# The seven products of the second channel product in transposed form, two of four sums per instruction, and small constants in shared space

## The chip, the cores and the metric

The kernel runs on one core of a Trainium2 chip (trn2). A core has a matrix engine (PE, with its weight loads shown apart as PEld), a vector engine (DVE), an engine for activation functions (ACT), a general engine (POOL), a queue engine (SP) and 16 DMA engines. The metric is the device time of one execution in microseconds (us); lower is better. A time is the median of several runs.

## What is computed

Two layers follow one another, for each of 8 batches (sequence S = 3008, width D = 256):

```
scores = (z @ z.T) / S                       # z: 3008 x 64
x  = u * (relu(scores)**2 @ v)               # u, v: 3008 x 256
h  = relu(x.T @ w_tok1) @ w_tok2             # w_tok1: 3008 x 256, w_tok2: 256 x 3008
u2 = x + h.T
out = u2 + relu(u2 @ w_ch1) @ w_ch2          # w_ch1: 256 x 1536, w_ch2: 1536 x 256
```

Inputs and output are float32 in memory; the products are taken in bf16 with float32 sums. The first channel product is `u2 @ w_ch1`, the second is `relu(...) @ w_ch2`.

## The kernel before

**Tiling.** The rows of a batch are cut into six blocks of 512 (the last has 448), called q; a block holds four tiles of 128 rows. Attention (`score_run`, `relu`, `square`, `av_matmul`) makes one block of scores after another: PE multiplies (L465), ACT takes the relu (L503), DVE squares (L511), and PE multiplies by v into `acc` (L692). Blocks of scores below the diagonal are not computed but obtained by turning the mirrored block with a transposing DMA on SP (L562, into buffers called `fl`). The result times u is `xT`.

**The mixer** of a batch (`add_mixer`) is a list of pieces: `tok1` (L1031) and `tok2` (L1105) for the token layer, `ch1` (L1162) for the first channel product, six pieces per block, each with 4 matmuls of 512 columns and one relu of 1024 columns on ACT (L1201) into `h2pre`, and `product` (L1298) for the second channel product.

**Seven products in place of eight.** The second channel product and the first token product use a scheme in which a 2x2 grid of sub-blocks is multiplied with seven products rather than eight, with sums of sub-blocks formed beforehand. For the second channel product the grid is: two interleaved sets of hidden columns (r) by two interleaved sets of row tiles (m). `make_sums` (L1227) forms, for each group d of four hidden tiles (three groups per block), four sums of relu outputs in `hsum`, each 512 elements per partition, with four DVE instructions: kind 0 (L1241), kind 2 (L1250), kind 1 (L1246, from kind 0), kind 3 (L1253, from kind 1). `mix_weights` (L975) forms four sums of w_ch2 once, in `w_mix_sb`. Each of the seven products is twelve matmuls of 128 columns (six where the block is short), into one of two PSUM banks: products 1, 6, 7, 4 go one after the other into the bank `xb`, and 2, 5, 3 into `zb`. After each, `collect` adds the bank to the output tile `ro` on DVE (L1334); products 6, 7, 4 wait for the addition of 1, 6, 7, and 5, 3 wait for that of 2, 5. Product 5 needs sum kind 0, 6 kind 1, 7 kind 2 and 3 kind 3; 1, 2 and 4 use plain relu outputs. For the token product `x_sums` (L904) forms four sums of x per block with four DVE instructions of 256 elements (L921); one of them overwrites part of x.

**Order of the work.** The program writes every engine's instruction order out by hand. A planner in the kernel (`push`, `run_engines`, the loop at the end) keeps a clock for PE, ACT, DVE and SP with an assumed cost for each operation, and takes at each step the piece that could start first; buffers are counted in `live` and `ROOM` (11 of `fl`, 6 of `h2`). Within a block the pieces of the second product are woven with the first product of the next block in the order 0, 0, 1, 2, 0, 6, 5, 0, 7, 3, 0, 4, where 0 is a `ch1` piece. The operations take their engine's queue in that order at run time, and PE executes in order: a matmul that waits holds all behind it. In the fourth block of all batches but the last the sums of two groups are held back (`late_sums`) and released together.

**Buffers the change touches.** `hsum` lies in an `fl` buffer (in early blocks an `at` buffer) and is given back after product 7. `a_f`, the token layer's first result in float32, lies in an `fl` buffer that is given back as soon as its relu is in `a_sb`, a constant tile. `ident`, a unit matrix for turning tiles on PE in the first 20 us, and `zs`, in which z is loaded, are constant tiles.

Of the kernel before, what the change touches and what calls it, by code (L numbers as in the profile page):

```python
# [57 lines left out]
def kernel(  # L58
# [38 lines left out]
    mark = consts.tile([P, 32], F32)  # L97
# [83 lines left out]
    def turn_on_pe(zr, zp):  # L181

        for t in range(GK):
            nc.tensor.matmul(  # L184
                zp[:, t, :], zr[:, t].rearrange("p h d -> p (h d)"), ident[:],
                start=(t == 0), stop=True, skip_group_check=True)
# [15 lines left out]
    def fill(n, bank):  # L202

        for _ in range(n):
            nc.tensor.matmul(
                bank, zero[:, :P], zero[:], start=True, stop=True, skip_group_check=True)
# [672 lines left out]
    def turn_x(b, q, t):  # L879

        if q % 2 == 0:
            x_pairs[b, q] = new_pair("fl" if b else "h2", [DT, QW // P, P], "x_pair")
        x = x_pairs[b, q - q % 2][:, q % 2]
        nc.sync.dma_start_transpose(
            out=x.rearrange("p h t d -> p (h t) d"),
            in_=xTs[b, q].rearrange("p h s -> p (h s)"))
        xs[b, q] = x
        x_done[b, q].t = t
        slack = 1.0 if b or q == NQ - 1 else 4.0 if q == NQ - 2 else 13.0
        push("dve", t + slack, 0.21, 0.36, lambda t: x_sums(b, q, t), first=-1,  # L890
             room=sums_room(b, q), frees=fl_free if xd_home(b, q) == "fl" and q % 2 == 0 else ())
# [16 lines left out]
    def x_sums(b, q, t):  # L908


        if q % 2 == 0:
            d_pairs[b, q] = new_pair(xd_home(b, q), [3, QW // P // 2, P], "d_pair")
        d = d_pairs[b, q - q % 2][:, q % 2]
        xds[b, q] = d
        v = xs[b, q].rearrange("p n (j r) d -> p n j r d", r=2)
        low, high = v[:, :, :, 0, :], v[:, :, :, 1, :]
        steps = [(d[:, 1], high[:, 1], low[:, 1]), (low[:, 1], low[:, 1], low[:, 0]),
                 (d[:, 0], high[:, 1], low[:, 1]), (d[:, 2], high[:, 0], d[:, 0])]

        def step(t):  # L920
            nc.vector.tensor_sub(*steps.pop(0))  # L921
# [52 lines left out]
    def mix_weights(t):  # L974


        w2 = w_ch2_sb.rearrange("p (j r) (h d) -> p j r h d", r=2, d=P)
        n = CHT // 4
        steps = []
        for c in range(2):  # L980
            low, high = w2[:, c * n:c * n + n, 0], w2[:, c * n:c * n + n, 1]
            to = w_mix_sb[:, :, c * n:c * n + n, :]
            steps += [
                (to[:, 0], low[:, :, 1, :], low[:, :, 0, :]),
                (to[:, 2], high[:, :, 1, :], low[:, :, 1, :]),
                (to[:, 1], high[:, :, 1, :], to[:, 0]),
                (to[:, 3], high[:, :, 0, :], to[:, 1])]

        def step(t):
            nc.vector.tensor_sub(*steps.pop(0))  # L990
# [4 lines left out]
        step(t)  # L995

    BORROW = 3
    VERY_LAST = (B - 1, NQ - 1, CHT // 2 - 1)
    ORDER_LAST = ((1, 2, 6, 5, 7, 0, 3, 4), (1, 2, 6, 5, 0, 7, 3, 0, 4))

    def add_mixer(b):
# [6 lines left out]
        def tok1(q, end):  # L1008
# [10 lines left out]
            for i in range(n):  # L1019
                j = q * n + i  # L1020
                products = [
                    ((0, 0), w[:, j, 0, 0, :], xp[:, 0, i, 0, :]),
                    ((0, 1), w[:, j, 1, 0, :], xp[:, 0, i, 1, :]),
                    ((1, 1), w[:, j, 0, 1, :], xp[:, 1, i, 0, :]),
                    ((0, 2), w_sum_sb[:, 1, j, :], d[:, 0, i, :]),
                    ((1, 2), w_sum_sb[:, 0, j, :], d[:, 1, i, :]),
                    ((0, 3), w_sum_sb[:, 2, j, :], xp[:, 1, i, 1, :]),
                    ((1, 0), w[:, j, 1, 1, :], d[:, 2, i, :]),
                ]
                for (r, k), lhs, rhs in products:  # L1030
                    nc.tensor.matmul(  # L1031
                        a_ps[:, r, k, :], lhs, rhs, start=(j == 0 and (r, k) in ((0, 0), (1, 1))),
                        stop=(j == KT // 2 - 1), skip_group_check=True)
# [3 lines left out]
            if q == NQ - 1:  # L1037
                home = "fl" if b else "h2"

                def collect_a(t):  # L1040
# [35 lines left out]
                    def relu_a(m, t):  # L1076
# [7 lines left out]
                        if len(made) == 2:  # L1084
                            recent[0] = to[:, :1]
                            if b:
                                release("fl", [1], max(made))
                            else:
                                live["h2"] -= 1

# [8 lines left out]
        def tok2(q, end):  # L1099
# [9 lines left out]
            def add(t):  # L1109
# [13 lines left out]
                u_done[q].t = t  # L1123
                st["turned", q] = push("sp", t, 1.25, 5.5, lambda t: turn_u2(q, t), first=1,
                                       room=lambda: has_room(("us",)) and (
                                           q <= HALF or goal[0] > (b, 1 + HALF)))
            ring.append((push("dve", end + 0.21, 1.12, 1.25, add, first=2), slot))

# [20 lines left out]
        def ch1(q, c2, borrowed, end):  # L1149
# [64 lines left out]
            if c2 == CHT // 2 - 1:  # L1214
                release("xT", xT_uses[q])

# [4 lines left out]
        def tiles_of(q, d, r, m):  # L1221

            n = pairs_of(q)
            return st["h2", q, d].rearrange("p (j r) w -> p j r w", r=2)[
                :, :, r, :2 * n * P].rearrange("p j (i m s) -> p j i m s", m=2, s=P)[:, :, :, m, :]

        def make_sums(q, d, t):  # L1227
# [6 lines left out]
            def kind(k):  # L1234
                return sums["s"][:, k, :, :n, :]

            def add1(t):
                home, n_home = take_home(q)
                sums["s"] = sb.tile([P, 4, 2, 2, P], BF16, tag=home, name="hsum", bufs=n_home)
                st["sum", q, d] = sums["s"]  # L1240
                nc.vector.tensor_add(kind(0), tiles_of(q, d, 0, 1), tiles_of(q, d, 1, 1))  # L1241
                push("dve", t - 0.05, busy, busy + 0.15, add3, done=s_done[q, d, 2])
                push("dve", t, busy, busy + 0.15, add2, done=s_done[q, d, 1])

            def add2(t):
                nc.vector.tensor_sub(kind(1), kind(0), tiles_of(q, d, 0, 0))  # L1246
                push("dve", t, busy, busy + 0.15, add4, done=s_done[q, d, 3])

            def add3(t):
                nc.vector.tensor_sub(kind(2), tiles_of(q, d, 0, 0), tiles_of(q, d, 0, 1))  # L1250

            def add4(t):
                nc.vector.tensor_sub(kind(3), tiles_of(q, d, 1, 0), kind(1))  # L1253

            push("dve", t, busy, busy + 0.15, add1, room=(home_of(q),), frees=frees_of(q),
# [16 lines left out]
        def product(q, k, end):  # L1272
# [6 lines left out]
            if k == 2:  # L1279
# [6 lines left out]
            weights = {1: w2[:, :, 0, 0, :], 2: w2[:, :, 1, 0, :], 3: w2[:, :, 1, 1, :],  # L1286
                       4: w_mix_sb[:, 3], 5: w_mix_sb[:, 0], 6: w_mix_sb[:, 1],
                       7: w_mix_sb[:, 2]}[k]
            first_use = k in (1, 2, 5)
            for c2 in range(CHT // 2):  # L1290
                d, j = divmod(c2, 2)
                for i in range(n):
                    if k in raw:
                        r, m = raw[k]
                        lhs = tiles_of(q, d, r, m)[:, j, i, :]
                    else:
                        lhs = st["sum", q, d][:, mixed[k], j, i, :]
# [6 lines left out]
            if k == 7:  # L1304
# [4 lines left out]
        def collect(q, k, end):  # L1309
# [6 lines left out]
            def res(m, h):  # L1316
                return st["res", q].rearrange("p (i m) d -> p i m d", m=2)[
                    :, :n, m, h * P:(h + 1) * P]

            def us(m, h):  # L1320
                return st["u", q][:, h, :2 * n, :].rearrange(
                    "p (i m) s -> p i m s", m=2)[:, :, m, :]
# [134 lines left out]

        def halves(q):
# [22 lines left out]
        def add_product(q, k):  # L1481
# [4 lines left out]
            kind = {5: 0, 6: 1, 7: 2, 3: 3}.get(k)  # L1486
# [16 lines left out]
        for q in range(NQ):  # L1503
            while added[q] < CHT // 2:
                add_next(q, q)
            rest = [(half, i) for half in halves(q) for i in range(pieces_of(q, half))]
            if fast(q):
                us_uses[q][0] += bool(rest)
                h2_uses[q] += bool(rest)
                for k in ORDER_LAST[b % 2] if q == NQ - 1 else (0, 0, 1, 2, 0, 6, 5, 0, 7, 3, 0, 4):  # L1510
                    if k:
# [56 lines left out]
    zero = sb.tile([P, QW], BF16, tag="h2", name="zero", bufs=ROOM["h2"])  # L1568
    nc.vector.memset(zero[:], 0.0)
# [121 lines left out]
    def first_u(landed):  # L1691
# [3 lines left out]
        def turn(end):  # L1695
            slot, _ = take_slot()
            up = bank_pair(slot, "up").rearrange("p r (t s) -> p (r t) s", s=P)
            for i in range(QW // P * DT):
                t, h = divmod(i, DT)
                nc.tensor.matmul(  # L1700
                    up[:, i, :], ur[:, t, h * P:(h + 1) * P], ident[:],
# [220 lines left out]
```

## Time and profile before

| what | value |
|---|---|
| median of 3 runs | 1112.31 us (1112.16 to 1115.65) |
| span of the profiled execution, first to last instruction | 1110.5 us |
| PE busy | 1105.7 us of the span, 11073 matmuls |
| DVE busy | 782.5 us, 1888 instructions |
| ACT busy | 669.4 us, 843 instructions |
| POOL busy | 164.3 us, 382 instructions |
| granted PE clock | 1.000 |

The profiled execution's span is 1.8 us shorter than the median of the timed runs, which also count what lies around the instructions. In the profile a row of a group gives its line in the kernel, its engine and operation, what is written and read, how often it runs, its busy time and mean duration, and the engine's idle time before it with what ended that.

### The profile page before, as it was taken

How to read it: one execution, taken by the hardware profiler on the slowest of the kernel's cores; microseconds unless marked ns; L12 is line 12 of the kernel's file. 1: busy time of each engine (PE TensorE's matmuls, PEld its weight loads, DVE VectorE, ACT ScalarE, POOL GpSimd, SP SyncE). 2: the span in 40 equal slices, each digit the busy share in tenths (PEclk: the TensorE clock that was granted, in tenths of full speed). 3: DMA queues.
4: the chain of work that ended last, by engine and by line, in shares of the span. 5: the costliest groups of instructions: out<-in, count | busy, mean ns of one | idle time of the engine just before them, and what ended most of it. 6: DMA issues, size and time to landing. Idle time of an engine off the chain costs nothing.

```text
span 1110.5 us, 27244 instructions
## 1 busy us (share of the span) xinstructions
PE 1105.7 (100%) x11073; PEld 683.8 (62%) x11073; DVE 782.5 (70%) x1888; ACT 669.4 (60%) x843; POOL 164.3 (15%) x382
## 2 busy tenths in 40 slices
PE   9999999999999999999999999999999999999998
PEld 3444575766557665576556865557655676556676
DVE  6889865975758857588566885578756777556775
ACT  7999555645854567545665456653666536743454
POOL 5320110221003110032100311003210120000100
PEclk9999999999999999999999999999999999999999
DMA  9999947796977969779697797967979678693222
GB/s 177 155 194 164 192 98 143 141 174 134 191 133 141 180 148 174 133 147 203 135 183 119 131 214 139 172 123 152 202 154 170 111 148 182 127 164 93 67 58 96
DMA packets 465725, 165.54 MB, mean 149 GB/s; under 512 B 433024, under 2 KB 448960, under 8 KB 465600
## 3 DMA queue, kind: packets, MB, share of 16 engines
q1 hardware_dynamic: 436208, 131.11, 58.6%
q0 software_dynamic: 28880, 32.32, 21.2%
q8 instruction: 86, 1.41, 0.5%
q10 hardware_dynamic: 512, 0.38, 0.1%
q14 instruction: 39, 0.32, 0.1%
HBM read 65.40 MB, written 24.64 MB: 81 GB/s over the span
## 4 chain that ended last, share of the span: by engine, by line
PE 99%; DMA 1%; issue 0%; POOL 0%; DVE 0%; POOLq 0%
PE acc L692 42%; PE hp L1162 22%; PE xb L1298 11%; PE zb L1298 8%; PE sc L465 6%; PE h_ps L1105 4%; PE a_ps L1031 3%; PE op L1398 2%; PE first_acc L609 1%; DMA v_sb<-in_v_dram 1%; PE zp L184 0%; PE up L1700 0%; DVE res L1433 0%; POOL ident masks.py:199 0%; POOL ident masks.py:197 0%
## 5 line engine op out<-in xcount | busy, mean ns | idle before, releaser
L1201 ACT ACTIVATE h2pre<-hp 128x1024 bf16<-128x1024 f32 (+1 forms) x287 | 278.5, 1008 | 204.0 <-PE hp L1162 171.5
L692 PEld LDWEIGHTS <-v_sb 64*128 64x128 bf16 x4418 | 246.3, 94 | 210.9
L692 PE MATMUL acc<-at,v_sb 64*128 64x512 bf16 (+1 forms) x2738 | 340.9, 375 | 0.0
L503 ACT ACTIVATE at<-sc 128x1024 bf16<-128x1024 f32 (+1 forms) x290 | 286.6, 1027 | 62.5 <-PE sc L465 54.8
L1162 PE MATMUL hp<-xT,w_ch_sb 128*128 128x512 bf16 (+1 forms) x1152 | 274.7, 375 | 0.0
L511 DVE TENSOR_TENSOR at<-at 128x1024 bf16<-128x1024 bf16 (+1 forms) x290 | 198.2, 687 | 103.8 <-ACT at L503 99.9
L692 PE MATMUL acc<-fl,v_sb 64*128 64x512 bf16 (+1 forms) x1680 | 192.5, 367 | 0.0
L1162 PEld LDWEIGHTS <-w_ch_sb 128*128 128x128 bf16 x1152 | 105.6, 98 | 98.1 <-issue 3.0
L1298 PEld LDWEIGHTS <-hsum 128*128 128x128 bf16 x2088 | 124.4, 98 | 18.2 <-issue 0.3
L465 PE MATMUL sc<-zT 64*128 64x512 bf16 (+1 forms) x732 | 131.8, 359 | 0.2 <-ACT zT L1750 0.2
L1298 PEld LDWEIGHTS <-h2pre 128*128 128x128 bf16 x1566 | 95.5, 98 | 20.1
L820 ACT COPY cp<-acc 128x512 f32<-128x512 f32 (+1 forms) x94 | 54.9, 584 | 77.8 <-PE acc L692 66.8
L826 DVE TENSOR_TENSOR cp<-acc,cp 128x512 f32<-128x512 f32 (+1 forms) x94 | 63.5, 676 | 50.7 <-ACT cp L820 50.1
L1241 DVE TENSOR_TENSOR hsum<-h2pre 128x512 bf16<-128x512 bf16 (+1 forms) x141 | 56.1, 402 | 40.7 <-ACT h2pre L1201 39.4
L491 ACT ACTIVATE at<-sc 128x512 bf16<-128x512 f32 (+3 forms) x152 | 56.2, 447 | 41.5 <-PE sc L465 41.0
L1298 PE MATMUL xb<-w_mix_sb,hsum 128*128 128x128 bf16 x1044 | 73.7, 219 | 0.0
L1334 DVE TENSOR_TENSOR ro<-xb,u_sb 128x256 f32<-128x256 f32 (+1 forms) x141 | 56.5, 401 | 22.5 <-PE xb L1298 20.5
L542 DVE TENSOR_TENSOR at<-at 128x512 bf16<-128x512 bf16 (+3 forms) x152 | 41.5, 321 | 38.2 <-ACT at L491 38.2
L465 PEld LDWEIGHTS <-zT 64*128 64x128 bf16 x732 | 42.8, 94 | 41.2 <-issue 3.6
L124 POOL CAST mark<-at 128x1 f32<-128x1 bf16 x24 | 8.2, 342 | 372.5 <-DVE at L511 372.5
L846 DVE TENSOR_TENSOR xT<-cp,uT 128x512 bf16<-128x512 f32 (+1 forms) x94 | 62.5, 665 | 0.9
L1253 DVE TENSOR_TENSOR hsum<-h2pre,hsum 128x512 bf16<-128x512 bf16 (+1 forms) x141 | 56.6, 401 | 2.3
(89 smaller groups left out, 968.4 us busy)
## 6 DMA issues: line engine op xcount, KB each, us to landing
out_dram<-ro SPq DMA_DIRECT2D x40, 512.0 KB, 3.0
v_sb<-in_v_dram POOLq DMA_DIRECT2D x40, 256.0 KB, 4.6
ur<-in_u_dram POOLq DMA_DIRECT2D x40, 256.0 KB, 4.9
w_tok_sb<-in_moe_w_tok_dram POOLq DMA_DIRECT2D x10, 256.0 KB, 10.7
zs<-in_z_dram POOLq DMA_DIRECT2D x35, 64.0 KB, 3.8
at<-at SPq DMA_TRANSPOSE x114, 2.4
out_dram<-ro SPq DMA_DIRECT2D x7, 256.0 KB, 3.5
fl<-at SPq DMA_TRANSPOSE x105, 4.7
```

The source lines that it names most:

```text
L465: nc.tensor.matmul(sc[:, r, c0:c1], zT[h, k:k + P], zT[h, m + c0:m + c1], start=True, stop=True)
L491: nc.scalar.activation(a3[:, i, c0:c1], sc[:, r, c0:c1], ACT.Relu, scale=inv_S)
L503: nc.scalar.activation(view, sv, ACT.Relu, scale=inv_S)
L511: nc.vector.tensor_mul(view, view, view)
L692: nc.tensor.matmul(o, vs[blk.b, g][rows, i, dh * P:(dh + 1) * P], rhs, start=(dh, h) not in blk.begun, stop=stop, skip_group_check=True)
L826: nc.vector.tensor_add(cp[:, :W], acc[:, 0, :W], cp[:, :W])
L846: nc.vector.tensor_mul(xT[:, dh, :full * P].rearrange("p (t s) -> p t s", s=P), acc[:, :full * P].rearrange("p (t s) -> p t s", s=P), uT[: ...
L1162: nc.tensor.matmul(hps[r % len(hps)][:, r, :W], w_ch1_sb[:, dc, cc * P:(cc + 1) * P], xT[:, dc, :W], start=(dc == 0), stop=(dc == DT - 1))
L1201: nc.scalar.activation(h2[:, :, :W], hp[:, :, :W], ACT.Relu)
L1253: nc.vector.tensor_sub(kind(3), tiles_of(q, d, 1, 0), kind(1))
L1298: nc.tensor.matmul(to[:, i * P:(i + 1) * P], lhs, weights[:, c2, :], start=(first_use and c2 == 0 and i == 0), stop=(c2 == CHT // 2 - 1), ...
L1334: nc.vector.tensor_add(res(m, h), source, us(m, h) if opening else res(m, h))
```

## The change

1. **Second channel product.** The seven products are paired the other way round (rows and hidden columns change places in the scheme). Products 1, 2 and 3 take plain relu outputs; 5, 7, 6 and 4 take sum kinds 0, 1, 2 and 3. Kinds 0 and 1 are now differences of the same form and are made by one instruction of 1024 elements; kinds 2 and 3 follow, each from the one before. The row tiles of a set m are now neighbours, not interleaved. `hsum` is given back after product 4, the last, rather than after 7. `mix_weights` forms the four weight sums that fit.
2. **Sums of x.** Two of the four are one instruction of 512 elements; none overwrites x. The buffer holds four sums rather than three.
3. **Space.** `zs` and `w_mix_sb` share one tile with room for `w_hid_sb`; `ident` lies beside `zero` in an `h2` buffer; `a_sb` lies in the last quarter of `a_f`, whose `fl` buffer is given back after the last `tok2` piece; `mark` shrinks from 32 to 8 columns.
4. **Code that is not reached.** A grouped form of the first channel product is added (`token_quarters`, `grouped_ch1`, `add_grouped`, `hidden_weights`), but the function `grouped` that chooses it returns False, and `hidden_weights` is not called.

```diff
-    w_mix_sb = consts.tile([P, 4, CHT // 2, P], BF16)
-    ident = consts.tile([P, P], BF16)
-    zs = consts.tile([P, KT + 2, d_qk], BF16)
+    HID, MIX = 8 * P, 4 * (CHT // 2) * P
+    shared_sb = consts.tile([P, HID + KT * d_qk + MIX], BF16)
+    w_mix_sb = shared_sb[:, HID + KT * d_qk:].rearrange("p (k c d) -> p k c d", k=4, d=P)
+    zs = shared_sb[:, HID - d_qk:HID + (KT + 1) * d_qk].rearrange("p (t d) -> p t d", d=d_qk)
...
-        steps = [(d[:, 1], high[:, 1], low[:, 1]), (low[:, 1], low[:, 1], low[:, 0]),
-                 (d[:, 0], high[:, 1], low[:, 1]), (d[:, 2], high[:, 0], d[:, 0])]
+        steps = [(d[:, 0:2], v[:, 1].rearrange("p j r d -> p r j d"), low),
+                 (d[:, 2], high[:, 1], d[:, 0]), (d[:, 3], high[:, 0], d[:, 2])]
...
-                        st["a"] = sb.tile([P, 2, D], BF16, tag="a", name="a_sb", bufs=1)
+                        st["a"] = f[:, 6:8, :].rearrange("p k d -> p (k d)").bitcast(
+                            BF16).rearrange("p (m d) -> p m d", m=2)
...
             ring.append((push("dve", end + 0.21, 1.12, 1.25, add, first=2), slot))
+            if q == NQ - 1:
+                if b:
+                    release("fl", [1], end + 0.2)
+                else:
+                    live["h2"] -= 1
...
+        def grouped(q, d=0):
+
+            return False
...
             def add1(t):
-                nc.vector.tensor_add(kind(0), tiles_of(q, d, 0, 1), tiles_of(q, d, 1, 1))
-                push("dve", t - 0.05, busy, busy + 0.15, add3, done=s_done[q, d, 2])
-                push("dve", t, busy, busy + 0.15, add2, done=s_done[q, d, 1])
+                h = quarters(q, d)
+                nc.vector.tensor_sub(sums["s"][:, 0:2, :, :n * P], h[:, :, 1], h[:, 0])
+                s_done[q, d, 1].t = t
+                push("dve", t - 0.05, busy, busy + 0.15, add2, done=s_done[q, d, 2])
...
-            raw = {1: (0, 0), 2: (1, 0), 4: (1, 1)}
-            mixed = {5: 0, 6: 1, 7: 2, 3: 3}
+            raw = {1: (0, 0), 2: (1, 0), 3: (1, 1)}
+            mixed = {5: 0, 7: 1, 6: 2, 4: 3}
...
             if k == 4:
                 done_with_h2(q)
-            if k == 7:
                 for d in range(CHT // 4):
                     release(home_of(q), [1], end + 0.2)
...
-            blocks_of = {1: (0, 0), 2: (0, 0), 5: (1, 1), 6: (0, 1), 3: (0, 1), 7: (1, 1),
-                         4: (1, 0)}
+            blocks_of = {1: (0, 0), 2: (0, 0), 5: (1, 1), 6: (1, 0), 3: (1, 0), 7: (1, 1),
+                         4: (0, 1)}
...
-    zero = sb.tile([P, QW], BF16, tag="h2", name="zero", bufs=ROOM["h2"])
+    zero_ident = sb.tile([P, QW + P], BF16, tag="h2", name="zero", bufs=ROOM["h2"])
+    zero, ident = zero_ident[:, :QW], zero_ident[:, QW:]
```

More of the change, by code (lines that the diff above doesn't have):

```diff
@@ L5 @@
 from concourse import bass_utils, mybir
+from concourse.dve_ops import TENSOR_ADD_SAT
 from concourse._compat import with_exitstack
@@ L205, in fill @@
             nc.tensor.matmul(
-                bank, zero[:, :P], zero[:], start=True, stop=True, skip_group_check=True)
+                bank, zero[:, :P], zero, start=True, stop=True, skip_group_check=True)
     def load_v(b, c):
@@ new lines, in grouped_ch1, with half, fork, keep @@
+        def grouped_ch1(q, d, stage, end):
+            xT = xTs[b, q]
+            x = xT.rearrange("p k (m n) -> p k m n", m=2)
+            w1 = w_ch1_sb[:, :, 4 * d * P:4 * (d + 1) * P].rearrange(
+                "p k (j r c) -> p r k j c", r=2, c=P)
+            T = st["T", q]
+            if stage == 0:
+                st["g_slot", q, d], _ = take_slot()
+                st["g", q, d] = bank_pair(st["g_slot", q, d], "gp")
+                live["h2"] += 1
+                st["h2", q, d] = sb.tile(
+                    [P, 4, QW], BF16, tag="h2", name="h2pre", bufs=ROOM["h2"])
+            ps = st["g", q, d]
+            s5 = st["s5", q]
+            h = st["h2", q, d].rearrange("p k w -> p (k w)").rearrange(
+                "p (r m n) -> p r m n", r=2, m=2)
+            products = [
+                [(0, w1[:, 0, 0], x[:, 0, 0], True), (1, w_hid_sb[:, 0], T[:, 0], True)],
+                [(1, w1[:, 0, 1], x[:, 1, 0], False), (0, w_hid_sb[:, 1], T[:, 2], False)],
+                [(0, w_hid_sb[:, 3], x[:, 1, 1], False), (1, w_hid_sb[:, 2], T[:, 1], False)],
+                [(1, w1[:, 1, 1], T[:, 3], False)]][stage]
+            for r, lhs, rhs, begins in products:
+                for j in range(2):
+                    nc.tensor.matmul(
+                        ps[:, r, j * 2 * P:(j + 1) * 2 * P], lhs[:, j, :], rhs,
+                        start=begins and j == 0, stop=True, skip_group_check=True)
+            def half(r):
+                return ps[:, r]
+            def fork(t):
+                nc.scalar.copy(half(1), half(0))
+            def keep(t):
+                nc.scalar.copy(s5, half(1))
+                push("act", t - 0.16, 0.62, 0.78, fork, first=2, done=g_done[q, d, 0])
+            def relu_first(t):
+                nc.scalar.activation(h[:, 0, 0], half(1), ACT.Relu)
+                push("act", t - 0.16, 0.62, 0.78, fork, first=2, done=g_done[q, d, 1])
+            def relu_last(t):
+                nc.scalar.activation(h[:, 1, 0], half(1), ACT.Relu)
+                recent[0] = h[:, 1, 0, :1]
+                live["xT"] -= 2
+                if ("rest", q, d) in st:
+                    st.pop(("rest", q, d))(t)
+            def add_two(t):
+                nc.vector._custom_dve(
+                    TENSOR_ADD_SAT, out=h[:, :, 1, :], in0=ps,
+                    in1=s5.unsqueeze(1).to_broadcast([P, 2, QW]), s0=3.0e38, s1=0.0)
+                make_sums(q, d, t, last=h2_done[q, 2 * d])
+            at = end + 0.21
+            if stage == 0:
+                push("act", at, 0.62, 0.78, keep, first=2)
+            elif stage == 1:
+                push("act", at, 0.62, 0.78, relu_first, first=2)
+            elif stage == 2:
+                push("dve", at, 1.2, 1.34, add_two, first=2, done=g_done[q, d, 2])
+            else:
+                done = h2_done[q, 2 * d]
+                push("act", at, 0.62, 0.78, relu_last, first=2, done=done)
+                ring.append((done, st["g_slot", q, d]))
@@ L1230, in make_sums @@
+        def make_sums(q, d, t, last=None):
             n = pairs_of(q)
@@ L1505, in add_mixer @@
                 add_next(q, q)
+            if q + 1 < NQ and grouped(q + 1):
+                added[q + 1] = 2
             rest = [(half, i) for half in halves(q) for i in range(pieces_of(q, half))]
```

148 lines of the change are left out of this document (106 added, 42 removed).

## The prediction

> **What bounds the kernel now.** I read the page first: its busy shares, its chain, and then the list of who waited for whom.
>
> ```profile
> span 1110.5 us, 27244 instructions
> PE 1105.7 (100%) x11073; PEld 683.8 (62%) x11073; DVE 782.5 (70%) x1888; ACT 669.4 (60%) x843; POOL 164.3 (15%) x382
> ...
> PEclk9999999999999999999999999999999999999999
> ...
> PE 99%; DMA 1%; issue 0%; POOL 0%; DVE 0%; POOLq 0%
> ```
>
> PE is busy in 1105.7 of 1110.5 us, at the full clock in every slice, and the chain that ends last runs on PE for 99% of the span; DVE, whose work the change reshapes, holds 0% of it. What is left of PE's idle time is in the waits of PE:
>
> ```profile
> PE wp L205 <- DVE zero L1569: 1.2, 1, 1.2
> PE first_acc L609 <- DMA v_sb<-in_v_dram: 0.4, 1, 0.4
> PE sc L465 <- ACT zT L1750: 0.2, 1, 0.2
> ```
>
> All three belong to the first 9 us. No wait of a matmul for a sum or for the output addition is listed.
>
> A busy PE may still hide stalls, as ends of matmuls are modelled. So I look at the distances between starts, in a stretch of the second channel product (start, duration, what):
>
> ```profile
> 474.82 0.83 PE L1298 MATMUL xb<-w_ch_sb,h2pre 128*128 128x128 bf16 x12
> 475.49 0.83 PE L1298 MATMUL zb<-w_ch_sb,h2pre 128*128 128x128 bf16 x12
> 476.16 1.03 PE L1162 MATMUL hp<-xT,w_ch_sb 128*128 128x512 bf16 x4
> 477.02 0.83 PE L1298 MATMUL xb<-w_mix_sb,hsum 128*128 128x128 bf16 x12
> 477.69 0.83 PE L1298 MATMUL zb<-w_mix_sb,hsum 128*128 128x128 bf16 x12
> 478.36 1.03 PE L1162 MATMUL hp<-xT,w_ch_sb 128*128 128x512 bf16 x4
> 479.23 0.83 PE L1298 MATMUL xb<-w_mix_sb,hsum 128*128 128x128 bf16 x12
> 479.90 0.83 PE L1298 MATMUL zb<-w_ch_sb,hsum 128*128 128x128 bf16 x12
> ```
>
> Twelve matmuls of 128 columns take 0.67 us whichever product it is, 55.8 ns each; four of 512 take 0.86 to 0.87 us, 216 ns each. A hidden stall would make one product longer than another. The same sum for the whole run: products and `ch1` in the chain are
>
> ```profile
> by line: PE acc L692 42.2%; PE hp L1162 22.0%; PE xb L1298 10.6%; PE zb L1298 7.9%; PE sc L465 6.5%; PE h_ps L1105 3.7%; PE a_ps L1031 3.4%; PE op L1398 1.7%; PE first_acc L609 1.0%; DMA v_sb<-in_v_dram 0.6%; issue 0.0%; PE zp L184 0.0%; PE
> ```
>
> 18.5% of 1110.5 is 205.4 us for the 3654 matmuls of L1298 (the code issues 40 full blocks of 84 and 7 short ones of 42), 56.2 ns each. Against 55.8 that leaves 1.5 us in 47 blocks. For L1162, 22.0% is 244.3 us; 960 matmuls at 216 ns and 192 of 448 columns, at seven eighths, are 243.7. So about 2 us at most is hidden in the pieces that the change could serve.
>
> [...]
>
> **The change part by part.**
>
> *PE.* I compared the built instruction order of the two kernels. Both have 11073 matmuls of the same shapes; what differs in the products is which tile is the weight and which the moving operand's source (products 3 and 4 change between relu tile and sum tile), at 55.8 ns either way. The grouped first product is not in it: the choosing function returns False. The order is the same but for one place, some 90 matmuls in batch 0 that lie at about 75 to 87 us of the span, where pairs of score matmuls stand up to eight `acc` matmuls (about 0.9 us) earlier or later. PE's and ACT's work there:
>
> ```profile
> 70.00:90.00 20.00, 20.00 (x204) 9.97 (x202) 18.05 (x39) 17.79 (x22) 1.14 (x3) 1.00 1.13 168
> ...
> 76.87 8.34 ACT L503 ACTIVATE at<-sc 128x896 bf16<-128x896 f32 x9 [0.41 <-PE sc L465]
> ```
>
> (Windows: PE, PEld, DVE, ACT, POOL busy.) ACT has a queue of nine relus there and works on without a gap, so a pair of scores that comes 0.9 us later finds ACT still busy. I cost it at 0; without that cover it is at most 0.9 us, once. PE: 0 us.
>
> *DVE, sums.* Rows by shape:
>
> ```profile
> L511 DVE TENSOR_TENSOR at<-at 128x1024 bf16<-128x1024 bf16 x278 | 190.8, 690 | 102.1 <-ACT at L503 98.4 <-DMA fl<-at 0.2
> ...
> L1241 DVE TENSOR_TENSOR hsum<-h2pre 128x512 bf16<-128x512 bf16 x120 | 50.1, 422 | 26.5 <-ACT h2pre L1201 26.2
> L1114 DVE TENSOR_TENSOR xT<-xT,h_ps 128x1024 bf16<-128x1024 bf16 x40 | 47.5, 1217 | 4.3 <-PE h_ps L1105 3.9
> ...
> L921 DVE TENSOR_TENSOR d_pair<-x_pair 128x256 bf16<-128x256 bf16 x96 | 25.5, 289 | 0.1
> ```
>
> and their distances in the queue, which are shorter than the durations, since one starts before the last has ended:
>
> ```profile
> 8.46 1.27 DVE L511 TENSOR_TENSOR at<-at 128x1024 bf16<-128x1024 bf16 x2
> ...
> 148.96 0.42 DVE L1250 TENSOR_TENSOR hsum<-h2pre 128x512 bf16<-128x512 bf16 x1
> 149.30 0.42 DVE L1246 TENSOR_TENSOR hsum<-hsum,h2pre 128x512 bf16<-128x512 bf16 x1
> 149.75 0.42 DVE L1253 TENSOR_TENSOR hsum<-h2pre,hsum 128x512 bf16<-128x512 bf16 x1
> ...
> 479.74 0.90 DVE L921 TENSOR_TENSOR d_pair<-x_pair 128x256 bf16<-128x256 bf16 x4
> ```
>
> A 512 takes 0.34 us of the queue, 0.45 before an instruction that reads its result (149.30 to 149.75); a 1024 takes 1.27 - 0.69 = 0.58; a 256 takes (0.90 - 0.29)/3 = 0.20. Four sums were 4 x 0.34 = 1.36 us, or 1.47 with that one wait. Now 0.58 + 2 x 0.34 = 1.26, or, where all three stand side by side, 0.69 + 0.03 + 0.45 + 0.34 = 1.51, as each reads the one before. That is between -0.10 and +0.04 us for each of 120 groups. Sums of x: 4 x 0.20 = 0.80 becomes 0.34 + 2 x 0.20 = 0.74, times 48. In all DVE gains at most 15 us of its 782.5, over the run, or loses 2; I take some 10. Fewer instructions, 141 + 48 = 189. Each such gain lies beside PE, so it is worth 0.
>
> The new 1024 instruction is not in the trace of before. Its bounds are the two rows of that width: 0.69 (bf16 in and out, in SBUF) and 1.22 (L1114, one input in PSUM). It reads and writes bf16 in SBUF, as L511 does, so I take 0.69. [...]
>
> *Does a later addition hold PE?* This is where it could cost. The tightest stretch I found is the block whose sums were held back. DVE is full there:
>
> ```profile
> 475.53 0.42 DVE L1241 TENSOR_TENSOR hsum<-h2pre 128x512 bf16<-128x512 bf16 x1
> 475.86 0.29 DVE L921 TENSOR_TENSOR d_pair<-x_pair 128x256 bf16<-128x256 bf16 x1
> 476.07 0.42 DVE L1250 TENSOR_TENSOR hsum<-h2pre 128x512 bf16<-128x512 bf16 x1
> 476.40 0.42 DVE L1334 TENSOR_TENSOR ro<-xb,u_sb 128x256 f32<-128x256 f32 x1
> 476.73 0.42 DVE L1246 TENSOR_TENSOR hsum<-hsum,h2pre 128x512 bf16<-128x512 bf16 x1
> 477.07 0.42 DVE L1334 TENSOR_TENSOR ro<-zb,ro 128x256 f32<-128x256 f32 x1
> ```
>
> Product 6 starts at 477.02 and needs the addition of product 1, over at 476.40 + 0.42 = 476.82: a margin of 0.20 us. Its ninth matmul, at 477.02 + 8 x 0.056 = 477.47, needs the last group's kind 1, over at 477.15: 0.32. Product 5, at 477.69, needs the addition of product 2, over at 477.49: 0.20. In the built order of after the same place holds: kinds 0 and 1 (1024), a sum of x (512), addition of 1, kind 2, addition of 2. From the same 475.53, with 0.58 for the wide sum and 0.34 for each of the others: the sum of x starts at 476.11, the addition of 1 at 476.45 (over at 476.87), kind 2 at 476.79 (over at 477.21), the addition of 2 at 477.13 (over at 477.55). Margins: 0.15, 0.26 and 0.14. They shrink by 0.05 and remain. Further along the sum kinds come earlier than before: 7 needs kind 1, now made with kind 0, and 3 none. In the other blocks the margin is wider: at 149.30 + 0.42 = 149.72 the last kind 1 is over, and the product that uses it starts after 151.2. Cost: 0.
>
> *Buffers.* `hsum` is held until product 4 instead of 7, about 2.2 us longer (0.67 + 0.87 + 0.67, by the PE rows). `a_f` is held to the last `tok2`. Chain and queue at that place in batch 2:
>
> ```profile
> 363.76 1.31 PE op L1398 x12
> ...
> 372.31 0.76 PE h_ps L1105 x4
> ...
> 403.74 0.67 PE xb L1298 x12
> 404.41 3.56 PE acc L692 x32
> ...
> 373.77 7.13 SPq L562 DMA_TRANSPOSE fl<-at  x3
> ```
>
> The relu into it is over near 364, the last `tok2` near 373: some 9 us longer, once per batch. What could queue for it is the turning of blocks into `fl`, issued on SP from 373.77 on, after the new release; the first `acc` that could use them is at 404.41, 30 us later, so a delay of 9 us is covered. SP's order differs in one exchange of two transposes in batch 0, and POOL's not at all; no DMA is added. `ident` and `zs` change only their address: the waits of their readers in the built order are for the same engines and queues. 0 us. If a buffer were the last one free, a sum would wait up to 2.2 us: a rival.
>
> *The sum:* PE 0, DVE -10 beside PE, buffers 0. Span 1110.5, as before; with the 1.8 us that the median stands above it, **1112.3 us**.
>
> **The rivals.**
>
> 1. *The wide sum runs at 1.22 us, and PE stands behind it: slower.* It is 0.53 longer. The margins of about 0.15 in the held-back block are then overrun by 0.38 by product 6, and again by the next wide sum ahead of the additions of 6 and 5: about 0.8 us in a batch, 7 batches, 6 us, and little elsewhere, where 1.5 us are free. 1118 us. It decides from 0.15 us. [...] Chance 0.04.
> 2. *A buffer runs short: slower.* A sum that waits 2.2 us for `fl` overruns the 0.26 by about 2 us; once a batch, 8 batches, 16 us: 1128. For it: fl buffers also hold flipped blocks and x. Against it: the built order of SP and POOL stands as it was, and in before DVE's idle time ahead of L1241 is the wait for ACT in 26.2 of 26.5 us. Chance 0.03.
> 3. *Hidden stalls go: faster.* At most the 2 us found above: 1110.3, still within 0.3%. To gain more, PE would have to issue less, and it issues the same. Chance of over 0.3%: 0.03.
> 4. *It does not do what it says.* The built order shows the transposed products and the wide sums, so no; only the grouped product is absent, and it is not claimed.
>
> **How the numbers follow.** About 0.3%, 3.3 us, is what a measurement of this kernel can tell from no change. The forecast, within it, has 0.90; rivals 1 and 2 make slower 0.07, rival 3 faster 0.03. The range holds the forecast alone, which is over 8 in 10: down by the 2 us of hidden stalls to 1110.3, and up to 1115.7, the highest of the three runs of before.
>
> **What would show it.** Right: PE's chain 99% with the same shares by line; DVE about 772 us with 189 instructions fewer; wide sums at 0.69; no wait of L1298 among PE's waits. Wrong: a wide sum over 1 us; a product of twelve over 0.67 us from start to start; idle time of DVE before its sums ended by a DMA. The forecast fails if PE shows waits in the mixer at all.

## The result and the profile after

The changed kernel takes 1126.8 us (median of four runs, 1123.83 to 1136.57) against 1112.44 us for the kernel before: a ratio of 1.014, 95% interval 1.0095 to 1.0186. It is slower, above the stated range. The profiled execution has a span of 1122.0 us. The first lines of its page:

```profile
span 1122.0 us, 26957 instructions
...
PE 1105.0 (98%) x11000; PEld 683.2 (61%) x11073; DVE 776.1 (69%) x1699; ACT 668.3 (60%) x843; POOL 169.6 (15%) x382
...
PE 90%; DMA 4%; DVE 2%; ACT 2%; issue 1%; SPq 0%; ACTq 0%; POOL 0%; DVEq 0%
```

PE has the same busy time as before (73 of its matmuls are missing from the records, the weight loads are complete), DVE 6.4 us less with 189 instructions fewer, and still the span grew by 11.5 us: the chain, 99% PE before, now runs 4% of the span through DMA and 5% through DVE, ACT and issue. So PE waits. Its list of waits:

```profile
PE sc L470 <- ACT at L508: 4.0, 4, 2.7
PE acc L697 <- DMA fl<-at: 2.3, 1, 2.3
PE wp L210 <- DVE zero L1730: 1.2, 1, 1.2
PE sc L470 <- ACT at L496: 1.0, 2, 0.6
PE xb L1447 <- DVE ro L1480: 0.4, 1, 0.4
```

All but the last, and the start's, sit in attention and not in the channel products. The scores (`sc`) wait for ACT, and ACT's own list says for what ACT waits:

```profile
ACT at L508 <- DMA fl<-at: 11.8, 7, 4.0
```

That is the turning of a block into `fl`, from here on called a flip. A flip reads the `at` buffer that a later relu on ACT is to fill, so a late flip holds ACT, and ACT holds the scores on PE. The kernel before has no wait of a relu for a flip. Two places of the chain, the token product of batch 0 and the last matmuls (start, duration, what), before:

```profile
110.65 4.80 PE a_ps L1031 x84
...
1102.21 5.25 PE op L1398 x48
```

and after:

```profile
117.19 4.80 PE a_ps L1058 x84
...
1113.62 5.25 PE op L1544 x48
```

6.5 us are lost by the end of batch 0, and 4.9 more in several places after it. By stages, first of before and then of after (the columns are the stage, its length, then PE, PEld, DVE, ACT and POOL busy, then PE's clock, DMA share, GB/s):

```profile
100.00:110.00 10.00, 10.00 (x96) 4.55 (x94) 8.50 (x19) 8.80 (x10) 1.04 (x2) 1.00 1.13 181
110.00:120.00 10.00, 10.00 (x135) 6.93 (x132) 7.45 (x15) 6.01 (x9) 0.71 (x2) 1.00 1.22 205
```

```profile
100.00:110.00 10.00, 7.56 (x70) 3.78 (x66) 6.60 (x14) 4.64 (x6) 1.91 (x2) 1.00 1.16 163
110.00:120.00 10.00, 6.57 (x84) 4.53 (x82) 5.13 (x8) 5.57 (x7) 0.00 (x0) 1.00 1.10 204
```

PE stands for 5.9 of these 20 us of after, and ACT and DVE are less busy than before as well. The chain of waits names what PE stands for at the first of its stalls there (start, duration, what):

```profile
95.49 0.60 DVE at L516
96.09 6.46 DMA fl<-at
102.55 0.04 issue
102.60 1.04 PE acc L697 x8
```

It is a flip again, this time one whose result PE itself needs. The share that the hardware's DMA queue takes of the 16 engines' time points to the reason. Before (packets, MB and share; then transposing DMAs, count and median us from issue to landing):

```profile
q1 hardware_dynamic: 436208, 131.11, 58.6%
...
fl<-at SPq DMA_TRANSPOSE x105, 4.7
...
uT<-ur SPq DMA_TRANSPOSE x47, 3.4
```

and after:

```profile
q1 hardware_dynamic: 436208, 131.11, 63.6%
...
fl<-at SPq DMA_TRANSPOSE x105, 5.1
...
uT<-ur SPq DMA_TRANSPOSE x47, 3.9
```

The same 436208 packets and the same 131.11 MB take 9.7% more of the engines' time (63.6% of 1122.0 us against 58.6% of 1110.5), and every kind of transposing DMA that runs more than twice lands later at the median. Nothing in the change adds a DMA, and on SP one pair changes places. What the change does alter is where tiles lie. In the built programs a later tile starts, in bytes of a partition:

```
             before     mod 512     after      mod 512
mark         16512                  16512
w_tok1       16640      256         16544      160
fl           154624     0           156064     416
ur           166912     0           168352     416
at           171008     0           172448     416
xT           199680     0           201120     416
```

`mark` shrinks from 128 to 32 bytes, and all that follows is 96 bytes short of the old grid (the other changes in space are multiples of 256).

### The profile page after: what moved, and what is told of

Same layout as the page of the kernel before. It is cut to its first block, busy times and chain, and to the rows that moved or that the text cites. A ratio compares the mean times of both kernels' runs of the same rounds, so it can differ in the third digit from the quotient of the medians.

```text
span 1122.0 us, 26957 instructions
## 1 busy us (share of the span) xinstructions
PE 1105.0 (98%) x11000; PEld 683.2 (61%) x11073; DVE 776.1 (69%) x1699; ACT 668.3 (60%) x843; POOL 169.6 (15%) x382
## 3 DMA queue, kind: packets, MB, share of 16 engines
q1 hardware_dynamic: 436208, 131.11, 63.6%
## 4 chain that ended last, share of the span: by engine, by line
PE 90%; DMA 4%; DVE 2%; ACT 2%; issue 1%; SPq 0%; ACTq 0%; POOL 0%; DVEq 0%
PE acc L697 36%; PE hp L1192 21%; PE xb L1447 10%; PE zb L1447 8%; PE sc L470 6%; PE h_ps L1128 4%; DMA fl<-at 3%; PE a_ps L1058 3%; PE op L1544 2%; ACT at L508 1%; PE first_acc L614 1%; DVE at L516 1%; DMA out_dram<-ro 0%; DMA v_sb<-in_v_dram 0%; ACT cp L825 0%
## 5 line engine op out<-in xcount | busy, mean ns | idle before, releaser
L1192 PE MATMUL hp<-xT,w_ch_sb 128*128 128x512 bf16 (+1 forms) x1089 | 271.3, 374 | 3.3
L1447 PEld LDWEIGHTS <-hsum 128*128 128x128 bf16 x2088 | 127.9, 98 | 28.8 <-issue 0.9
L1383 DVE TENSOR_TENSOR hsum<-h2pre 128x1024 bf16<-128x1024 bf16 (+1 forms) x141 | 91.1, 650 | 43.5 <-ACT h2pre L1231 33.9
L831 DVE TENSOR_TENSOR cp<-acc,cp 128x512 f32<-128x512 f32 (+1 forms) x94 | 63.6, 677 | 48.0 <-ACT cp L825 47.2
L1447 PE MATMUL xb<-shared_sb,hsum 128*128 128x128 bf16 x1044 | 73.6, 219 | 0.4 <-DVE ro L1480 0.4
```

Source lines behind the costliest of these rows:

```text
L831: nc.vector.tensor_add(cp[:, :W], acc[:, 0, :W], cp[:, :W])
L1192: nc.tensor.matmul(hps[r % len(hps)][:, r, :W], w_ch1_sb[:, dc, cc * P:(cc + 1) * P], xT[:, dc, :W], start=(dc == 0), stop=(dc == DT - 1))
L1383: nc.vector.tensor_sub(sums["s"][:, 0:2, :, :n * P], h[:, :, 1], h[:, 0])
L1447: nc.tensor.matmul(to[:, i * P:(i + 1) * P], lhs, weights[:, c2, :], start=(first_use and c2 == 0 and i == 0), stop=(c2 == CHT // 2 - 1), ...
```

## The experiments

**Theory A**: tiles off their grid make the transposing DMAs slower, flips come late, and PE waits. **Rivals**: B, the longer hold of `a_f` and `hsum` in `fl` buffers delays the flips; C, the changed order on DVE, and the place in batch 0 where scores moved, stall PE. Ratios below are to runs of the kernel before on the same chip, with 95% intervals.

### The address alone

The changed kernel put back on the grid (the unused room for weights of the grouped product is halved to make place):

```diff
-    mark = consts.tile([P, 8], F32)
+    mark = consts.tile([P, 32], F32)
-    HID, MIX = 8 * P, 4 * (CHT // 2) * P
+    HID, MIX = 4 * P, 4 * (CHT // 2) * P
```

> The changed kernel with the marker tile at its old 32 columns and the room for the unused weights of the grouped product halved, so that every later tile starts at a multiple of 512 bytes again, as in the kernel before; instructions and their order are those of the changed kernel. Theory A (addresses: tiles that start 416 bytes past a multiple of 512 make the transposing DMAs slower, and late flips stall PE): 1111 to 1113 us, hardware DMA queue back at 58 to 59% of the span, flips landing in 4.7 us at the median. Rival B (buffers: the fl buffers of a_f and hsum are held longer and delay the flips): no change from the changed kernel, 1122 to 1130 us. Rival C (order: the wider sums on DVE and the moved scores in batch 0 stall PE): 1122 to 1130 us.

1117.95 us, 1.0046 (1.0031 to 1.0061). The profiled span is 1113.2 us.

```profile
q1 hardware_dynamic: 436208, 131.11, 58.4%
...
PE 97%; DVE 1%; DMA 1%; ACT 0%; issue 0%; POOL 0%; ACTq 0%
```

The queue is back to the share of before, and some two thirds of the loss are gone, against B and C as sole causes. But not all: 0.46% is left, which A does not explain, and the 1111 to 1113 us expected from A alone are missed.

The kernel before, taken off the grid, with nothing else changed:

```diff
-    mark = consts.tile([P, 32], F32)
+    mark = consts.tile([P, 8], F32)
```

> The kernel before with only the marker tile cut from 32 to 8 columns, which moves every later tile down by 96 bytes, to 416 past a multiple of 512; nothing else changes. Theory A: the whole loss, 1122 to 1130 us, hardware DMA queue at 63 to 64%. Rivals B and C: 1112 us, queue at 58.6%.

1127.9 us, 1.0131 (1.0108 to 1.0155).

```profile
q1 hardware_dynamic: 436208, 131.11, 64.4%
...
PE 85%; DMA 8%; DVE 4%; ACT 2%; issue 1%; SPq 0%; ACTq 0%; DVEq 0%
```

One number in one line, the size of a tile of which a single column is used, makes the loss of the whole change. A is shown.

### Which grid

The same line of the kernel before with 48, 64 and 96 columns, so that later tiles lie 64, 128 and 256 bytes past a multiple of 512.

> The kernel before with the marker tile at 48 columns: every later tile lies 64 bytes past a multiple of 512. Theory A with a grain of 256 or 512 bytes: slow, 1120 to 1130 us, queue at 62 to 64%. Theory A with a grain of 64 bytes: 1112 us, queue at 58.6%. Rivals B and C: 1112 us.

> The kernel before with the marker tile at 64 columns: every later tile lies 128 bytes past a multiple of 512. If a row read that does not start at a multiple of 256 bytes is cut in two, whatever the distance: as at 64 and at 416 past, queue 63 to 64.5%, 1122 to 1130 us. If the grain is 128 bytes: 1112 to 1113 us, queue 58 to 59%.

> The kernel before with the marker tile at 96 columns: every later tile lies 256 bytes past a multiple of 512. Theory A with a grain of 256 bytes or less: 1112 us, queue at 58.6%. Theory A with a grain of 512 bytes: 1120 to 1130 us. Rivals B and C: 1112 us.

64 past: 1125.95 us, 1.0121 (1.0106 to 1.0136), queue

```profile
q1 hardware_dynamic: 436208, 131.11, 63.6%
```

128 past: 1126.21 us, 1.0118 (1.007 to 1.0167), queue

```profile
q1 hardware_dynamic: 436208, 131.11, 64.1%
```

256 past: 1112.76 us, 1.0004 (0.9994 to 1.0013), queue

```profile
q1 hardware_dynamic: 436208, 131.11, 58.2%
```

The grid is 256 bytes by these runs, and at the three places tried off it the price hardly depends on how far: 63.6% at 64, 64.1% at 128, 64.4% at 160 past (416 past a multiple of 512 is 160 past one of 256). The times say the same: 1.0004 at 256 past, 1.0118 to 1.0131 at 64, 128 and 160. That a row read is cut in two, as the expectation of the run at 128 past has it, was the author's supposition and is not shown: how the queue cuts its reads is in none of these traces.

### Which side pays

Padding in the kernel before that shifts the destination of the flips, then their source, then the sources of the other three kinds. The `fl` buffers off by 64 (later ones by 256, which cost nothing above); these buffers also take most output tiles and sums, most turned x, and 4 of the 48 `ur` and `uT`, which move with them:

```diff
+    sb.tile([P, 32], BF16, tag="pad0", name="pad0", bufs=1)
     load_v(0, 0)
+    sb.tile([P, 96], BF16, tag="pad1", name="pad1", bufs=1)
```

> The kernel before with 64 bytes of padding ahead of the fl buffers and 192 behind them: the fl buffers alone (where flipped blocks, turned x and most sums are written) lie 64 past a multiple of 512, all earlier tiles stand at 0 and all later ones at 256, which cost nothing by the last run. If the writing side of a transposing DMA pays for its address: 1117 to 1126 us, flips landing in 5.0 us or more at the median, queue over 60%. If the reading side pays: 1112 to 1113 us, queue 58 to 59%, flips 4.7.

1113.52 us, 1.0013 (0.9995 to 1.003). The flips' time to landing, shortest, median and longest, in the kernel before and here:

```profile
DMA to landing us min/median/max: 3.6/4.7/8.3
```

```profile
DMA to landing us min/median/max: 3.6/4.6/10.9
```

The transfer itself is not slower. The time is not wholly free of the shift: three of the ten runs, the profiled one among them, stand near 1118 us, where the kernel before has two of 17 near 1116.7.

The `at` buffers off by 64:

```diff
+            fresh = not ready_at
+            if fresh:
+                sb.tile([P, 32], BF16, tag="pad0", name="pad0", bufs=1)
             ats[b, q, g] = sb.tile([P, GK * QW], BF16, tag="at", name="at", bufs=ROOM["at"])
+            if fresh:
+                sb.tile([P, 96], BF16, tag="pad1", name="pad1", bufs=1)
```

> The kernel before with 64 bytes of padding ahead of the at buffers and 192 behind them: the at buffers alone, from which flipped blocks are read (and in which the blocks on the diagonal are turned in place), lie 64 past a multiple of 512. If the reading side of a transposing DMA pays: 1117 to 1126 us, flips landing in 5.0 us or more at the median, queue over 60%. If the writing side pays: 1112 to 1114 us (the in-place blocks alone are written there), queue 58 to 60%.

1118.74 us, 1.0055 (1.0038 to 1.0073), the queue at 61.5%, and the same line for the flips:

```profile
DMA to landing us min/median/max: 4.3/5.0/8.9
```

The shortest flip, the one that queueing can have lengthened least, goes from 3.6 to 4.3 us when its source is off the grid and not at all when its destination is. The `ur` (44 of 48) and `xT` buffers off by 64, `at`, `fl` and `uT` on the grid:

```diff
+        if not urs and not uTs:
+            sb.tile([P, 32], BF16, tag="pad0", name="pad0", bufs=1)
         ur = sb.tile([P, QW // P, D], BF16, tag=tag, name="ur", bufs=n)
...
+            if not ready_at:
+                sb.tile([P, 96], BF16, tag="pad1", name="pad1", bufs=1)
             ats[b, q, g] = sb.tile([P, GK * QW], BF16, tag="at", name="at", bufs=ROOM["at"])
...
+            if not xTs:
+                sb.tile([P, 32], BF16, tag="pad2", name="pad2", bufs=1)
             xTs[b, q] = sb.tile([P, DT, QW], BF16, tag="xT", name="xT", bufs=ROOM["xT"])
```

> The kernel before with padding so that the ur and xT buffers, from which the other three kinds of transposing DMA read (uT from ur, x_pair and u_sb from xT), lie 64 bytes past a multiple of 256; the at and fl buffers and uT stay at multiples of 256, and the output buffers behind xT are shifted with it. If the reading side pays whatever the tile: the rest of the loss in the queue's share, that is 60.5 to 61.5%, uT landing in 3.8 to 3.9 us at the median instead of 3.4, x_pair 4.0, flips 4.7; time 1113 to 1121 us. If at alone matters: queue 58 to 59%, 1112 to 1113 us.

1113.56 us, 1.0 (0.9989 to 1.0011), with

```profile
q1 hardware_dynamic: 436208, 131.11, 60.5%
...
uT<-ur SPq DMA_TRANSPOSE x47, 4.0
```

The flips stay at 4.7 us at the median. So the reading side of a transposing DMA pays, in each of the tiles tried: the shortest transfer goes from 3.6 to 4.3 us out of `at`, from 2.7 to 3.0 out of `ur`, and from 2.7 to 3.0 (`x_pair`) and 3.1 (`u_sb`) out of `xT`. The queue's times add up nearly: shares times spans are 651 us for before, 686 with `at` off (61.5% of 1115.9), 673 with `ur` and `xT` off (60.5% of 1111.8), 656 with `fl` off (58.8% of 1116.2), so 35 + 22 + 5, against 65 with everything off by 64 (63.6% of 1125.2). The runs' times do not: 0.55% for `at` and nothing for `ur` and `xT`, against 1.2 to 1.3% for all. The 22 us more for `ur` and `xT` alone do not show in the time, so what they feed must have had that slack. Why the whole is more than its parts was not tried.

### What is left: 0.46%

The kernel on the grid with the old four sums of x per block; its built order on PE, ACT and SP is then the old one, and the transposed product, the wide sum of relu outputs and all buffers stay as changed:

```diff
-        steps = [(d[:, 0:2], v[:, 1].rearrange("p j r d -> p r j d"), low),
-                 (d[:, 2], high[:, 1], d[:, 0]), (d[:, 3], high[:, 0], d[:, 2])]
+        steps = [(d[:, 1], high[:, 1], low[:, 1]), (low[:, 1], low[:, 1], low[:, 0]),
+                 (d[:, 0], high[:, 1], low[:, 1]), (d[:, 2], high[:, 0], d[:, 0])]
...
-        push("dve", t + slack, 0.34, 0.48, lambda t: x_sums(b, q, t), first=-1,
+        push("dve", t + slack, 0.21, 0.36, lambda t: x_sums(b, q, t), first=-1,
```

> The aligned form of the changed kernel (every later tile at a multiple of 512 bytes) with the old four sums of x per block; its built order on PE, ACT and SP is then that of the kernel before, while the transposed second product, its wider sum instruction and the buffers stay as changed. Theory C1 (what is left of the loss, 0.46%, comes from the changed order in batch 0 that the new sums of x bring with them): 1112 to 1113 us, no wait of a score for ACT. Rival B1 (it comes from the longer hold of a_f and hsum, or from the wider sums of relu outputs): 1116 to 1120 us, as the aligned form.

1113.09 us, 1.0003 (0.9994 to 1.0011): the time of before. The converse, the new sums of x alone put into the kernel before (the diff above the other way round; in both, the token product's operands and the sums' buffer go with it):

> The kernel before with the new three sums of x per block alone, addresses as before; the built order on PE, ACT and SP is then that of the changed kernel (48 places on PE, one exchange on ACT and one on SP). Theory C1: 1116 to 1120 us, PE short by 2 to 5 us between 88 and 112 us of the span. Rival B1: 1112 to 1113 us.

1118.68 us, 1.0058 (1.0038 to 1.0078). PE's only listed wait beyond the first microseconds, and then its stages, are

```profile
PE sc L465 <- ACT at L503: 2.0, 1, 2.0
```

```profile
100.00:110.00 10.00, 9.36 (x88) 4.18 (x85) 7.44 (x16) 6.25 (x7) 1.91 (x2) 1.00 1.12 166
110.00:120.00 10.00, 8.65 (x120) 6.38 (x121) 6.73 (x13) 6.21 (x9) 0.00 (x0) 1.00 1.22 202
```

So the rest comes with the sums of x. Is it the order that they bring, or the instruction? On the grid, all edits kept, and only the cost that the planner is told for the first sum put back, which gives the old order with the new instructions:

```diff
-        push("dve", t + slack, 0.34, 0.48, lambda t: x_sums(b, q, t), first=-1,
+        push("dve", t + slack, 0.21, 0.36, lambda t: x_sums(b, q, t), first=-1,
```

> The aligned form of the changed kernel with all its edits, the new sums of x among them, but the planner is told the old cost for the first sum of x (0.21 us in place of 0.34); the built order on PE, ACT and SP is then that of the kernel before. Theory C1, if the order itself is the cause: 1112 to 1113 us. If the wider sum of x on DVE is the cause and not the order: 1115 to 1120 us. Rival B1: 1116 to 1120 us.

1114.65 us, 1.0018 (1.001 to 1.0027). More than half of it was the order: 0.46% becomes 0.18%. What remains shows as small stalls in the held-back blocks. PE in that block of batch 4:

```profile
621.67 0.92 PE L1192 MATMUL hp<-xT,w_ch_sb 128*128 128x448 bf16 x4
622.62 0.83 PE L1447 MATMUL xb<-shared_sb,hsum 128*128 128x128 bf16 x12
623.29 0.83 PE L1447 MATMUL zb<-shared_sb,hsum 128*128 128x128 bf16 x12
623.96 0.92 PE L1192 MATMUL hp<-xT,w_ch_sb 128*128 128x448 bf16 x4
624.93 0.83 PE L1447 MATMUL xb<-shared_sb,hsum 128*128 128x128 bf16 x12
```

Four matmuls of 448 columns last 0.76 us from start to start elsewhere, and here 0.95 and 0.97: 0.2 us of waiting, twice. DVE in the same stretch shows for what:

```profile
619.88 1.29 DVE L926 TENSOR_TENSOR d_pair<-x_pair,d_pair 128x256 bf16<-128x256 bf16 x6
621.09 0.69 DVE L1383 TENSOR_TENSOR hsum<-h2pre 128x1024 bf16<-128x1024 bf16 x1
621.81 0.43 DVE L1388 TENSOR_TENSOR hsum<-h2pre,hsum 128x512 bf16<-128x512 bf16 x1
622.15 0.42 DVE L1480 TENSOR_TENSOR ro<-xb,u_sb 128x256 f32<-128x256 f32 x1
...
623.70 0.52 DVE L1383 TENSOR_TENSOR hsum<-h2pre 128x512 bf16<-128x512 bf16 x1 [0.47 <-ACT h2pre L1231]
...
624.46 0.42 DVE L1480 TENSOR_TENSOR ro<-xb,u_sb 128x256 f32<-128x256 f32 x1
```

The addition of the bank `xb` ends at 622.57, after the sums of x and the wide sum ahead of it; the next product in that bank was due at 622.43. The second time DVE stands 0.47 us for a relu of ACT with a wide sum at the head of its queue, and the addition behind it ends at 624.88; the next product was due at 624.72. With the old sums of x, and the order on DVE that goes with them, both stalls are absent. Whether the instruction's length or the changed order on DVE makes them was not separated.

Last, the old order at the changed kernel's addresses, by the same one line in the changed kernel:

> The changed kernel, addresses as it has them (416 past a multiple of 512), with the planner told the old cost of the first sum of x, so that the built order on PE, ACT and SP is that of the kernel before. If addresses and order add up: 1121 to 1124 us, that is the 1126.8 of the changed kernel less the 5 of the order. If the order costs only where transposes are quick: 1126 us.

The median of the six runs is 1129.18 us (1120.81 to 1137.81); without the longest it is 1127.64, and the ratio, taken from these five, is 1.0129 (1.0103 to 1.0155). This was a miss for adding up: off the grid the old order gives back nothing that the runs can tell. In its profiled execution, the shortest of the six (span 1119.0 us), the token product of batch 0 starts at 110.84 us, so the 6.5 us by the end of batch 0 are gone, and the time is lost in later batches.

## Why the prediction was wrong

**What bounds the kernel** was read rightly: PE, busy in 1105.7 of 1110.5 us, had no slack to give, and a change that leaves its work as it is could not gain more than the rest. What was read wrongly is the other direction, what such a change can lose. The sign named for it came, but small: PE waits 0.4 us for an addition in the mixer, and nearly all of PE's other waits stand in attention.

**The DVE terms held.** The wide sum took 0.69 us as priced, not 1.22 (rival 1):

```profile
L1383 DVE TENSOR_TENSOR hsum<-h2pre 128x1024 bf16<-128x1024 bf16 x120 | 82.2, 689 | 26.7 <-ACT h2pre L1231 23.1 <-DMA out_dram<-ro 1.9 <-PE xb L1447 1.5
```

DVE lost 6.4 us of busy time where some 10 were said. The margins in the held-back block were read as 0.15 us and enough; with the old order and the grid kept, about 0.2 us is overrun in them (the run at 1.0018). That step was close, and on the wrong side. With the old sums of x there is no such loss (1.0003), so the wide sum of relu outputs does not use the margin up by itself; the new sums of x have to come on top.

**The hold of buffers** was priced rightly: the longer hold of `a_f` and `hsum` costs nothing that shows (rival 2), as the run at 1.0003 has it in full.

**The step that failed** stands at the end of the paragraph on buffers: "`ident` and `zs` change only their address", priced at 0 us. Two things were missed. The address was taken as free, without asking who reads it; and only the tiles named in the diff were looked at, while `mark`, eight columns for 32, moves every tile behind it. The runs put 1.2 to 1.3% in its place, 13 to 15 us: every tile that a transposing DMA reads lay off the 256-byte grid, the queue took 10 to 12% longer for the same packets, and flips came late for ACT and PE. None of the four rivals had it, though the profile gave a hint: a DMA share of 1.13 already in the stage from 70 to 90 us that the prediction shows.

**The second failure** is the order in batch 0, priced at 0 and at most 0.9 us, with nine queued relus on ACT as cover. It cost 2.3 us in the profiled execution of the changed kernel on the grid (110.65 became 112.92 for the token product of batch 0). In the timed runs on the grid the order stands for the step from 0.46% to 0.18%, some 3 us. The cover was checked for the moved scores alone; what follows them (the relu, the square, the flip and the buffer that the flip frees) was not. The chain of that execution shows it: from 103.34 us on it hangs for 7.15 us on a flip, and the relu that waits for this flip holds the scores on PE, which wait 2.2 us. Whether the moved scores or the exchange of two transposes on SP, a `uT` ahead of a flip, does the harm was not separated.

The chance of 0.90 for no change rested above all on the built order being nearly equal. An equal order says that no planned wait was added; it does not say that each operation lasts as long.

## What to carry to other kernels

When a change resizes a tile, compare the start addresses of all later tiles, above all of those that transposing DMAs read: at a multiple of 256 bytes a source cost nothing here (1.0004), off it the queue took 10 to 12% more time for the same packets (63.6% of 1122.0 us to 64.4% of 1127.8, against 58.6% of 1110.5). Saved space should be given back as padding where it breaks the grid. This kernel, whose PE is always busy, had nothing to gain from less work elsewhere and over 1% to lose from transfers that land late, so price what feeds PE as carefully as what PE does.

## What the runs showed of the hardware that was not expected

The price of a source off the grid is in the single transfer: the shortest flip goes from 3.6 to 4.3 us, with the destination's address without effect (3.6).

A stall of PE can cost more than its own length. In the kernel before taken off the grid by 96 bytes, PE waits 4.65 us for an addition on DVE, behind a transfer of the output that holds the chain for 9.29 us. The stage ahead of the stall, the stall, what follows it, and the stage after that (columns as above, the clock third from the end):

```profile
895.00:906.60 11.60, 11.60 (x136) 8.58 (x134) 10.18 (x37) 6.63 (x7) 5.62 (x11) 1.00 1.25 127
906.60:911.27 4.67, 0.02 (x2) 0.00 (x1) 0.89 (x4) 0.92 (x1) 0.30 (x2) 0.83 1.29 213
911.27:916.69 5.42, 5.42 (x43) 4.51 (x43) 3.72 (x16) 0.92 (x1) 0.15 (x1) 0.52 0.19 30
916.69:921.40 4.71, 4.71 (x76) 4.22 (x74) 1.99 (x7) 0.92 (x1) 1.41 (x5) 1.00 0.71 166
```

The granted clock is full until the stall, falls within it, and is about half for the 5 us that follow, though PE is busy there without a gap: twelve matmuls of 128 columns hold the chain for 1.44 us from 911.27 on and twelve more for 1.28 us, in place of 0.67. So the stall comes first and the lower clock second, and together they cost some 7 us (4.65 of waiting, and 2.6 more for work that takes 2.8 at the full clock, 5.42 us at 0.52). In the kernel with only `fl` off, PE stands for 1.98 of the 10 us from 100 us on and is slow after that as well: eight matmuls of `acc` hold the chain for 1.71 us from 111.13 on, in place of 0.86, and the clock is 0.83 over the 10 us from 110 on. A wait of 2.72 us in the changed kernel (clock 1.00 from 115 to 120 us and from 120 to 125) and one of 2.2 us in its form on the grid (1.00 from 90 to 125 us, with the wait in it) are not followed by a lower clock, so the length of the wait alone does not decide it. Of the kernels with every later tile off the grid, the longest runs have a mean clock of 0.994 to 0.998, those of the kernel before 0.998 to 1.0, which fits stalls of this kind; of those runs only the one shown here was profiled.
